# Linear attention and a gated MLP in one kernel: a fourth buffer in a shared ring, 64-wide kv, px in quarters

## The chip, the cores and the metric

The kernel runs on one core of a Trainium2 chip. The metric is the device time of one execution in microseconds. The kernel before took 828.76 us (median of three runs, 827.92 to 829.11). Engines are named as in the profile: PE is TensorE (PEld its weight loads), DVE VectorE, ACT ScalarE, POOL GpSimd, SP SyncE, which issues nearly all DMAs.

## The reference

q, k and v are 8 batches x 8 heads x 576 positions x 64, in float32; the MLP goes from 512 to 2048 and back. Cut to what is computed:

```python
q_s = softmax(q, axis=-1)            # over the 64 of a head
k_s = softmax(k, axis=2)             # over the 576 positions
kv  = einsum('bhsd,bhse->bhde', k_s, v)      # 64 x 64 for each batch and head
x   = einsum('bhsd,bhde->bhse', q_s, kv)     # then 4608 tokens x 512
h   = x @ w_in
g   = h * clip(h + 3, 0, 6) / 6
out = g @ w_out
```

The attention is linear: `kv` is small, and each token's query multiplies the `kv` of its own batch and head.

## The kernel before

**Stages.** The 4608 tokens are handled as three blocks of 512 (j = 0, 1, 2) and then three super-blocks of 1024 (s = 0, 1, 2). Two heads always go together as a head pair (hp, four of them), with 2 x 64 = 128 partitions. Blocks run the MLP as two plain products: for each of 16 chunks of the hidden width, `gemm1` makes `ph`, relu6 makes `g`, and `gemm2` adds into four banks `po`; `store` (L770) empties these at a block's end, two on ACT (L781) and two on DVE (L779). A float32 value is split into a high and a low part, and each product is three fast passes (hi·hi, hi·lo, lo·hi). Super-blocks use a two-by-two scheme with seven products in place of eight, which needs sums and differences of weight blocks.

**Weights.** They arrive as raw words (`load_w`) and are decoded during block 0 by `decode` (L146): ACT and DVE steps through `m` into a tile `v`, then a split into a resident tile `w`. From chunk 6 on `v` is also stored to DRAM (`whole`, L166). During blocks 1 and 2 `sum_weights` (L482) takes a pair of chunks and a side (in or out) at a time: it fills a tile `w4` with the plain weights (from `w` for the first three pairs, L488, later by a load of `whole`, L491), writes the sums into a second tile `sums` (L497 to L500), splits both and stores four blocks to DRAM (`keep`, L469, seen as `wf<-v`). The generator `all_sums` has 26 steps; one is taken in each chunk from block 1's n = 4 on (`n > 3`).

**The ring `v`.** One ring of three buffers of 4 KB per partition, all under the name `v`, serves the decoded tile, `w4`, `sums`, block 2's output tiles (L773), the last relu6 of phase 1 (L626) and phase 2's output tiles (L662). A new tile waits until all readers of the one three back have finished, stores included.

**Attention.** For a batch and a head pair, `kv_of` (L207) forms `pkv` in PSUM (576 positions in 5 pieces, 2 heads, 64 columns of `v` and one of ones), takes the reciprocal of the sums and writes `kv`. For block 0, block 1, block 2 and super-block 0, `kv` is a 128x128 tile with the two heads' 64x64 on the diagonal and zeros elsewhere, made by one DVE instruction with a `mask` (L225). The product `px` with the turned queries `qT` is then one matmul of the whole array for each run of tokens of one batch. From super-block 1 on (`quarters`) `kv` is 64 wide (L221), and `px` is made of 64x64 matmuls on the four corners of the array: rows by head, columns by which 512 tokens, with a PSUM bank for each head (L421 to L435). A float32 matmul shows up as two instructions.

**Queries.** `attention` (L276) serves blocks 0 and 1. For block 1 the queries come into `qt`, are normalised there, turned on PE into PSUM (`tp`) and copied by ACT to a second tile `qT` (L298); both have one buffer. `token_attention` (L361) serves the rest; its queries come in a layout that DVE can turn (L350), into a tile also called `qt` (L384).

**Order.** A planner in the framework simulates the program while it is built and puts each engine's instructions in order; buffers that are not free yet are part of what it simulates. From block 1 on matmuls keep the order in which the program names them. `behind` ties work to come after the last relu6 or split that was issued. Attention for the next stage runs in small steps between the chunks (`steps`, L808): a list of units, a number of steps for each, and `shared`, the steps at which the unit before goes on too. Block 1's attention runs during block 0 with 3 steps a unit and `shared = (2,)`, so the previous unit's px comes with the present unit's `kv_of`. Engines and SP's queue run strictly in the order that they were given.

Of the kernel before, what the change touches and what calls it, by code (L numbers as in the profile page):

```python
# [33 lines left out]
def attention_moe(  # L34
# [62 lines left out]
    make_identity(nc, ident)  # L97
    mask = const.tile([P, P], F32, name="mask")
    nc.gpsimd.memset(mask, 0.0)
    nc.gpsimd.memset(mask[0:D, 0:D], 1.0)  # L100
    nc.gpsimd.memset(mask[D:P, D:P], 1.0)
    three = const.tile([P, 1], F32, name="three")
# [43 lines left out]
    def decode(f):  # L146

        n = 2 * DM
        pairs = raws.pop(f).rearrange("p (n two) -> p n two", two=2)
        low, high = pairs[:, :, 0], pairs[:, :, 1]  # L150
        m = moe.tile([P, n], F32, name="m", bufs=1)
        nc.scalar.activation(m, high.bitcast(F32), AF.Abs)
        nc.vector.tensor_scalar(m, m, W_MIN, W_MAX, op0=ALU.max, op1=ALU.min)
        m = m.bitcast(U32)
        nc.vector.tensor_scalar(
            m, m, 3, 0x3FFFFFFF, op0=ALU.logical_shift_left, op1=ALU.bitwise_and
        )
        v = moe.tile([P, n], F32, name="v", bufs=3)
        vu = v.bitcast(U32)
        nc.vector.scalar_tensor_tensor(  # L160
            vu, high, 0xC0000000, m, op0=ALU.bitwise_and, op1=ALU.bitwise_or
        )
        nc.scalar.activation(low, low, AF.Copy, scale=2.0**-29)
        nc.vector.tensor_tensor(vu, vu, low, op=ALU.add)
        if f // 2 >= FROM_DRAM:
            nc.sync.dma_start(whole[:, f], v)  # L166
        parts = place(f, F32R, f"w_{f}").rearrange("p (s i n) -> p s i n", s=2, i=2)
        split_ahead(
            parts[:, :, 0],
            parts[:, :, 1],  # L170
            v.rearrange("p (s n) -> p s n", s=2),
        )
        wi[f], wo[f] = parts[:, 0], parts[:, 1]
# [9 lines left out]
    kvs = {}  # L183
    narrow = set()

# [6 lines left out]

    first = {}

    def load_first(hp):
# [10 lines left out]

    def kv_of(hp, batches, quarters=False):  # L207
        n = len(batches)
        both = bank_a("pkv")[:, 0 : n * (D + 1)].rearrange("p (b d) -> p b d", b=n)
        for i, (_, ke, vt) in enumerate(batches):  # L210
            for c in range(NCH):
                for h in range(2):
                    hs = slice(h * D, (h + 1) * D)
                    mm(both[hs, i], ke[:, c, hs], vt[:, c, h, :], c == 0, c == NCH - 1, n > 1)
        rk = att.tile([P, 2], F32, name="rk", bufs=2)[:, 0:n]
        nc.vector.tensor_scalar_add(rk, both[:, :, D], EPS)
        nc.vector.reciprocal(rk, rk)
        for i, (b, _, _) in enumerate(batches):
            kv = att.tile([P, P], F32, name="kv", bufs=10)
            if quarters:  # L220
                nc.vector.tensor_scalar_mul(kv[:, 0:D], both[:, i, 0:D], rk[:, i : i + 1])  # L221
                kvs[b, hp] = kv
                narrow.add((b, hp))
                continue
            nc.vector.scalar_tensor_tensor(  # L225
                kv.rearrange("p (h d) -> p h d", h=2),
                both[:, i : i + 1, 0:D].broadcast_to([P, 2, D]),
                rk[:, i : i + 1],
                mask.rearrange("p (h d) -> p h d", h=2),
                op0=ALU.mult,  # L230
                op1=ALU.mult,
            )
            kvs[b, hp] = kv
# [42 lines left out]
    def attention(j, hp):  # L276

        if not j:
            kt, qt, qT, vt, ke = first[hp]
        else:  # L280
            kt = load_kt(j, hp)
            ke = att.tile([P, NCH, P], F32, name="ke", bufs=2)
            vt = load_v(j, hp)
            qt = att.tile([P, TB], F32, name="qt", bufs=1)
            nc.sync.dma_start(qt, q[j, hp])
            qt = qt.rearrange("p (c h d) -> p c h d", c=NC4, h=2)
        km = att.tile([P, 1], F32, name="km", bufs=2)
# [10 lines left out]
        nc.scalar.copy(qT, tp)  # L298
# [37 lines left out]
    def q_softmax_t(qt):  # L336
# [14 lines left out]
        return qT  # L351

    held = {}

# [6 lines left out]
    def token_attention(t0, n, hp, put):  # L361
# [39 lines left out]
        yield  # L401
        kv_of(hp, list(zip(new, ke, vt)), t0 >= START + SB)
        yield
# [7 lines left out]
    def sb_attention(s):  # L411
        def put(t0, hp, need, qT):

            if not s:
                for c in range(SB // TB):
                    px = bank_a("px")
                    for b, lo, hi in segments(need, t0 + c * TB):
                        mm(px[:, lo:hi], kvs[b, hp], qT[:, c * TB + lo : c * TB + hi], True, True)
                    nc.scalar.copy(x_of(s)[:, hp, c * TB : (c + 1) * TB], px)
                return  # L420
            px = [bank("px") for _ in range(2)]  # L421
            rows = [slice(h * D, (h + 1) * D) for h in range(2)]
            for both in zip_longest(*(segments(need, t0 + c * TB) for c in range(2))):
                for c, part in enumerate(both):
                    if part:
                        b, lo, hi = part
                        for h, r in enumerate(rows):
                            mm(
                                px[h][rows[c], lo:hi],
                                kvs[b, hp][r, slice(0, D) if (b, hp) in narrow else r],  # L430
                                qT[r, c * TB + lo : c * TB + hi],
# [10 lines left out]
    def block_attention(j):  # L442
        def put(t0, hp, need, qT):
            px = bank_a("px")
            for b, lo, hi in segments(need, t0):
                mm(px[:, lo:hi], kvs[b, hp], qT[:, lo:hi], True, True)
            x_hi, x_lo = x_block(j)
            split(x_hi[:, hp, :], x_lo[:, hp, :], px)
# [33 lines left out]
    def sum_weights(pair, side):  # L482

        w4 = moe.tile([P, 2 * DM], F32, name="v", bufs=3)
        if pair < FROM_DRAM:
# [8 lines left out]
        a11, a12, a21, a22 = (q1, q3, q2, q4) if side else (q1, q2, q3, q4)  # L494
        sums = moe.tile([P, 2 * DM], F32, name="v", bufs=3)
        s1, s3, s2, s4 = (sums[:, n * HT : (n + 1) * HT] for n in range(4))
# [85 lines left out]
    def phase1(s):  # L582
        xb, yb, zb = {}, {}, {}
        for i, (p, n) in enumerate(SLOTS1):
# [24 lines left out]
            with tc.high_priority():  # L609
# [14 lines left out]
                if n == 6:  # L624
                    nc.vector.tensor_add(h21, h21, y)
                    r = moe.tile([P, 2 * DM], F32, name="v", bufs=3)  # L626
                    relu6(gb, r, gb)
            yield

    def phase2(s):  # L630
# [30 lines left out]
        def outs(name):  # L661
            return moe.tile([P, 2 * DM], F32, name="v", bufs=3).rearrange("p (c n) -> p c n", c=2)  # L662

# [106 lines left out]
    def store(j, po):  # L770
        for t in range(NTT):
            if j == NB - 1:
                ob = moe.tile([P, 2 * DM], F32, name="v", bufs=3)[:, 0:DM]  # L773
            else:
# [66 lines left out]
    for j in range(NB):  # L841
        if j == 1:
            in_order.append(True)
        if j < NB - 1:
# [119 lines left out]
```

## Time and profile before

| | us |
|---|---|
| median of three runs | 828.76 |
| profiled execution, its own time | 827.1 |
| its span, first to last instruction | 825.3 |
| PE busy | 798.8 (97%) |
| DVE busy | 673.4 (82%) |
| ACT busy | 454.1 (55%) |
| POOL busy | 55.7 (7%) |

In the profile a line is that of the kernel's source, and a helper that records every matmul gives all matmuls one line (L88); they are told apart by `out<-in`, the names of the tiles. A shape such as `64*64 64x320` is the part of the array used and the moving data. A number in brackets after an instruction is the idle time of its engine just before it, and what ended that. Busy time of PE uses modelled ends of matmuls, so short idle times of PE do not show in it. The profile's clock is the share of full speed that TensorE was granted, 0.996 over the whole span.

### The profile page before, as it was taken

How to read it: one execution, taken by the hardware profiler on the slowest of the kernel's cores; microseconds unless marked ns; L12 is line 12 of the kernel's file. 1: busy time of each engine (PE TensorE's matmuls, PEld its weight loads, DVE VectorE, ACT ScalarE, POOL GpSimd, SP SyncE). 2: the span in 40 equal slices, each digit the busy share in tenths (PEclk: the TensorE clock that was granted, in tenths of full speed). 3: DMA queues.
4: the chain of work that ended last, by engine and by line, in shares of the span. 5: the costliest groups of instructions: out<-in, count | busy, mean ns of one | idle time of the engine just before them, and what ended most of it. 6: DMA issues, size and time to landing. Idle time of an engine off the chain costs nothing.

```text
span 825.3 us, 11783 instructions
## 1 busy us (share of the span) xinstructions
PE 798.8 (97%) x4088; PEld 641.3 (78%) x4088; DVE 673.4 (82%) x1064; ACT 454.1 (55%) x733; POOL 55.7 (7%) x155
## 2 busy tenths in 40 slices
PE   4899899999989999999999999999999999999998
PEld 3577678888877778887877788777788888888886
DVE  7998998589979888888999994798699836658873
ACT  7897673334444445556556653565556535445543
POOL 5000001010111110001003000011000000000000
PEclk9999999999999999999999999999999999999999
DMA  9999676245579873888786677775566776666673
GB/s 368 416 407 334 199 263 225 59 163 189 192 239 341 288 263 128 267 279 277 272 279 213 187 233 251 226 234 183 178 184 199 238 247 197 187 201 185 197 218 114
DMA packets 75803, 192.30 MB, mean 233 GB/s; under 512 B 7264, under 2 KB 19808, under 8 KB 73696
## 3 DMA queue, kind: packets, MB, share of 16 engines
q1 hardware_dynamic: 75024, 190.38, 70.1%
q10 hardware_dynamic: 720, 1.18, 0.4%
q8 instruction: 32, 0.52, 0.3%
q14 instruction: 27, 0.22, 0.1%
HBM read 147.49 MB, written 44.04 MB: 232 GB/s over the span
## 4 chain that ended last, share of the span: by engine, by line
PE 69%; DVE 16%; DMA 7%; ACT 4%; issue 3%; SPq 1%; POOL 1%; DVEq 0%; ACTq 0%; POOLq 0%
PE x L88 29%; PE z L88 11%; PE y L88 11%; PE ph L88 7%; PE po L88 7%; DMA wf<-v 4%; DMA qt<-in_qf_dram 2%; PE px L88 2%; DVE g L580 1%; PE pkv L88 1%; DVE v L160 1%; DVE qt L343 1%; DVE v L121 1%; DVE gp L121 1%; DVE m L350 1%
## 5 line engine op out<-in xcount | busy, mean ns | idle before, releaser
L121 ACT CAST gf<-g 128x512 fp32r<-128x512 f32 x168 | 104.2, 622 | 97.5 <-DVE gf L121 37.0
L88 PE MATMUL po<-w,gp 128*128 128x512 f32 x576 | 145.5, 399 | 3.6 <-DVE gp L779 2.1
L88 PE MATMUL ph<-x,w 128*128 128x512 f32 x576 | 142.7, 394 | 3.2 <-ACT w L121 2.0
L121 DVE TENSOR_TENSOR gf<-g,gf 128x512 fp32r<-128x512 f32 x168 | 112.9, 686 | 25.3 <-ACT gf L121 24.9
L88 PEld LDWEIGHTS ph<-x,w 128*128 128x128 f32 x576 | 107.8, 188 | 29.6 <-ACT w L121 3.0
L88 PEld LDWEIGHTS po<-w,gp 128*128 128x128 f32 x576 | 106.7, 189 | 29.2 <-DVE gp L779 2.5
L88 PE MATMUL x<-right,gp 128*128 128x512 f32 x384 | 94.6, 391 | 0.4 <-ACT g L616 0.4
L88 PE MATMUL x<-gf,gp 128*128 128x512 f32 x384 | 94.1, 390 | 0.0
L88 PEld LDWEIGHTS x<-gf,gp 128*128 128x128 f32 x384 | 71.9, 188 | 15.7 <-DVE gf L121 0.4
L88 PEld LDWEIGHTS x<-right,gp 128*128 128x128 f32 x384 | 71.6, 188 | 15.7 <-ACT g L616 0.8
L579 ACT ACTIVATE g<-ph,three 128x512 f32<-128x512 f32 x48 | 32.7, 684 | 38.1 <-PE ph L88 38.1
L88 PE MATMUL y<-right,gp 128*128 128x512 f32 x192 | 49.1, 391 | 0.0
L88 PE MATMUL x<-right,left 128*128 128x512 f32 x192 | 47.7, 392 | 0.0
L88 PE MATMUL x<-gf,left 128*128 128x512 f32 x192 | 47.0, 390 | 0.0
L88 PE MATMUL z<-gf,gp 128*128 128x512 f32 x192 | 46.9, 390 | 0.0
L333 POOL COPY swap<-qm 32x32 f32<-32x32 f32 (+1 forms) x64 | 19.6, 306 | 355.3 <-DVE qm L341 353.3
L121 ACT CAST gp<-g 128x512 fp32r<-128x512 f32 x48 | 29.7, 619 | 23.8 <-DVE g L580 23.7
L88 PEld LDWEIGHTS z<-gf,gp 128*128 128x128 f32 x192 | 36.0, 188 | 7.8 <-DVE gf L121 0.4
L88 PEld LDWEIGHTS x<-gf,left 128*128 128x128 f32 x192 | 35.9, 188 | 7.7 <-ACT v L702 0.2
L88 PEld LDWEIGHTS y<-right,gp 128*128 128x128 f32 x192 | 35.8, 188 | 7.6 <-issue 0.2
L88 PEld LDWEIGHTS x<-right,left 128*128 128x128 f32 x192 | 35.7, 188 | 7.6
L580 DVE SCALAR_TENSOR_TENSOR g<-g,ph 128x512 f32<-128x512 f32 x48 | 32.6, 680 | 9.2 <-ACT g L579 9.1
(139 smaller groups left out, 1279.8 us busy)
## 6 DMA issues: line engine op xcount, KB each, us to landing
gp<-wf SPq DMA_DIRECT2D x112, 512.0 KB, 4.2
left<-wf SPq DMA_DIRECT2D x56, 512.0 KB, 4.2
raw<-in_w_dram SPq DMA_DIRECT2D x16, 1024.0 KB, 13.6
wf<-v SPq DMA_DIRECT2D x64, 256.0 KB, 3.2
wf<-w SPq DMA_DIRECT2D x48, 256.0 KB, 4.5
vt<-in_v_dram SPq DMA_DIRECT2D x28, 325.0 KB, 5.6
kt<-in_kT_dram SPq DMA_DIRECT2D x28, 288.0 KB, 3.8
ke<-in_k_dram SPq DMA_DIRECT2D x24, 320.0 KB, 5.1
```

What stands on the lines that cost most here:

```text
L88: nc.tensor.matmul(out, lhsT, rhs, start=start, stop=stop, skip_group_check=goes_on)
L121: return nc.scalar.copy(hi, src), nc.vector.tensor_sub(lo, src, hi.bitcast(F32))
L160: nc.vector.scalar_tensor_tensor(vu, high, 0xC0000000, m, op0=ALU.bitwise_and, op1=ALU.bitwise_or)
L333: nc.gpsimd.tensor_copy(swap[r : r + QD], stat[o : o + QD])
L343: nc.vector.tensor_sub(qs, qs, across(qm))
L350: nc.vector.transpose(qT, qt)
L579: ahead(nc.scalar.activation(r, h, AF.Relu, bias=three, scale=1.0))
L580: ahead(nc.vector.scalar_tensor_tensor(g, r, 6.0, h, op0=ALU.min, op1=ALU.mult))
```

## The change

- The ring `v` has four buffers, at all seven places where it is named.
- Room for it: `mask` is gone; `kv` is 64 wide for every batch (ten tiles); `qT` of block 1 is gone. Its queries now come into half of a tile `qt` that is 1024 wide and shared with `token_attention` (kept in `held["q"]`, halves by turns of hp), and the turned queries are copied back to where they came from.
- `px` of all stages that used the whole array is made by the new function `heads`: two 64x64 matmuls for each run of tokens, rows and columns of one head, both into the same PSUM bank.
- Block 1's attention has `shared = (1,)`: the previous unit's px comes with the present unit's transposes.
- The sums of weights start one chunk earlier, at n = 3 of block 1 (`n > 2`).

```diff
-    mask = const.tile([P, P], F32, name="mask")
...
-        v = moe.tile([P, n], F32, name="v", bufs=3)
+        v = moe.tile([P, n], F32, name="v", bufs=4)
...
-    def kv_of(hp, batches, quarters=False):
+    def kv_of(hp, batches):
...
-            kv = att.tile([P, P], F32, name="kv", bufs=10)
-            if quarters:
...
-            nc.vector.scalar_tensor_tensor(
...
+            kv = att.tile([P, D], F32, name="kv", bufs=10)
+            nc.vector.tensor_scalar_mul(kv, both[:, i, 0:D], rk[:, i : i + 1])
             kvs[b, hp] = kv
...
-            qt = att.tile([P, TB], F32, name="qt", bufs=1)
-            nc.sync.dma_start(qt, q[j, hp])
-            qt = qt.rearrange("p (c h d) -> p c h d", c=NC4, h=2)
+            if "q" not in held:
+                held["q"] = att.tile([P, SB], F32, name="qt", bufs=1)
+            qT = held["q"][:, hp % 2 * TB : (hp % 2 + 1) * TB]
+            nc.sync.dma_start(qT, q[j, hp])
+            qt = cut(qT, 0, NC4, 2, D)
...
-        if j:
-            qT = att.tile([P, TB], F32, name="qT")
         nc.scalar.copy(qT, tp)
...
-                mm(px[:, lo:hi], kvs[b, hp], qT[:, lo:hi], True, True)
+                heads(px, lo, hi, kvs[b, hp], qT, True)
...
+    def heads(px, lo, hi, kv, qT, start):
+
+        for h in range(2):
+            r = slice(h * D, (h + 1) * D)
+            mm(px[r, lo:hi], kv[r], qT[r, lo:hi], start, True, True)
...
-                step = steps(units, 3, (2,))
+                step = steps(units, 3, (1,))
...
-            if j > 1 or j and n > 3:
+            if j > 1 or j and n > 2:
                 behind(sums)
```

The other puts (super-block 0, block 2) change in the same way as the one shown; those of super-blocks 1 and 2 keep their order and only lose the test for which kind of `kv` they read.

More of the change, by code (lines that the diff above doesn't have):

```diff
@@ L97, in attention_moe @@
     make_identity(nc, ident)
-    mask = const.tile([P, P], F32, name="mask")
-    nc.gpsimd.memset(mask, 0.0)
-    nc.gpsimd.memset(mask[0:D, 0:D], 1.0)
-    nc.gpsimd.memset(mask[D:P, D:P], 1.0)
     three = const.tile([P, 1], F32, name="three")
@@ L183, in attention_moe @@
     kvs = {}
-    narrow = set()
     def cut(t, at, *shape):
@@ L193, in attention_moe @@
     first = {}
+    held = {}
     def load_first(hp):
@@ L218, in kv_of @@
         for i, (b, _, _) in enumerate(batches):
-            kv = att.tile([P, P], F32, name="kv", bufs=10)
-            if quarters:
[L221 to L232, printed above, removed]
+            kv = att.tile([P, D], F32, name="kv", bufs=10)
+            nc.vector.tensor_scalar_mul(kv, both[:, i, 0:D], rk[:, i : i + 1])
             kvs[b, hp] = kv
@@ L351, in q_softmax_t @@
         return qT
-    held = {}
     def x_of(s):
@@ L401, in token_attention @@
         yield
-        kv_of(hp, list(zip(new, ke, vt)), t0 >= START + SB)
+        kv_of(hp, list(zip(new, ke, vt)))
         yield
@@ L417, in put @@
                     for b, lo, hi in segments(need, t0 + c * TB):
-                        mm(px[:, lo:hi], kvs[b, hp], qT[:, c * TB + lo : c * TB + hi], True, True)
+                        heads(px, lo, hi, kvs[b, hp], qT[:, c * TB : (c + 1) * TB], True)
                     nc.scalar.copy(x_of(s)[:, hp, c * TB : (c + 1) * TB], px)
@@ L429, in put @@
                                 px[h][rows[c], lo:hi],
-                                kvs[b, hp][r, slice(0, D) if (b, hp) in narrow else r],
+                                kvs[b, hp][r],
                                 qT[r, c * TB + lo : c * TB + hi],
@@ L445, in put @@
             for b, lo, hi in segments(need, t0):
-                mm(px[:, lo:hi], kvs[b, hp], qT[:, lo:hi], True, True)
+                heads(px, lo, hi, kvs[b, hp], qT, True)
             x_hi, x_lo = x_block(j)
@@ L482, in sum_weights @@
     def sum_weights(pair, side):
-        w4 = moe.tile([P, 2 * DM], F32, name="v", bufs=3)
+        w4 = moe.tile([P, 2 * DM], F32, name="v", bufs=4)
         if pair < FROM_DRAM:
@@ L494, in sum_weights @@
         a11, a12, a21, a22 = (q1, q3, q2, q4) if side else (q1, q2, q3, q4)
-        sums = moe.tile([P, 2 * DM], F32, name="v", bufs=3)
+        sums = moe.tile([P, 2 * DM], F32, name="v", bufs=4)
         s1, s3, s2, s4 = (sums[:, n * HT : (n + 1) * HT] for n in range(4))
@@ L625, in phase1 @@
                     nc.vector.tensor_add(h21, h21, y)
-                    r = moe.tile([P, 2 * DM], F32, name="v", bufs=3)
+                    r = moe.tile([P, 2 * DM], F32, name="v", bufs=4)
                     relu6(gb, r, gb)
@@ L661, in outs @@
         def outs(name):
-            return moe.tile([P, 2 * DM], F32, name="v", bufs=3).rearrange("p (c n) -> p c n", c=2)
+            return moe.tile([P, 2 * DM], F32, name="v", bufs=4).rearrange("p (c n) -> p c n", c=2)
         def send(t, r, c):
@@ L772, in store @@
             if j == NB - 1:
-                ob = moe.tile([P, 2 * DM], F32, name="v", bufs=3)[:, 0:DM]
+                ob = moe.tile([P, 2 * DM], F32, name="v", bufs=4)[:, 0:DM]
             else:
```

## The prediction

> **What bounds the kernel now.** I read the head of the page first, then busy time by stage, then who waited for whom, and last the timelines of the few places where TensorE stood still. The page:
>
> ```profile
> span 825.3 us, 11783 instructions
> PE 798.8 (97%) x4088; PEld 641.3 (78%) x4088; DVE 673.4 (82%) x1064; ACT 454.1 (55%) x733; POOL 55.7 (7%) x155
> ```
>
> The stages (start and end, length, then busy time and instructions of PE, PEld, DVE, ACT and POOL, granted clock, DMA share, GB/s); 34 to 130 is block 0 with its decoding, 130 to 232 block 1, 232 to 330 most of block 2, then the super-blocks:
>
> ```profile
> 0.00:34.00 34.00, 21.10 (x147) 16.00 (x148) 28.61 (x52) 26.61 (x39) 12.85 (x25) 0.95 0.97 386
> 34.00:130.00 96.00, 91.18 (x461) 69.76 (x460) 90.79 (x129) 73.54 (x149) 0.50 (x2) 0.98 0.86 310
> 130.00:232.00 102.00, 102.00 (x550) 82.64 (x549) 85.12 (x166) 42.81 (x68) 11.82 (x44) 1.00 0.48 155
> 232.00:330.00 98.00, 94.47 (x516) 76.30 (x515) 83.74 (x151) 44.84 (x70) 11.60 (x36) 1.00 0.76 259
> 330.00:825.00 495.00, 490.10 (x2421) 396.63 (x2419) 385.12 (x570) 266.33 (x411) 18.90 (x48) 1.00 0.70 219
> ```
>
> TensorE sets the end. In block 1 it never stops, so whatever is added to it there is paid and whatever another engine saves there is lost. It can gain 3.5 us in block 2 (98.00 less 94.47), 4.8 us in block 0, where VectorE with 90.79 of 96 is as much the bound, and little later. Who waited for whom (total, times, longest):
>
> ```profile
> PE po L88 <- DVE gp L779: 2.1, 1, 2.1
> DVE v L497 <- DMA wf<-v: 5.6, 3, 3.0
> PE px L88 <- DVE kv L225: 2.2, 2, 1.9
> ```
>
> The second row is the ring of the change: L497 writes the new sums tile `v`, and with three buffers it must wait until the stores `wf<-v` of the tile three back have landed. What such a wait does is seen on VectorE at the turn from block 1 to block 2, and on TensorE at the same time:
>
> ```profile
> 240.25 0.43 DVE L497 TENSOR_TENSOR v<-v 128x256 f32<-128x256 f32 x1 [2.95 <-DMA wf<-v]
> ...
> 240.93 1.24 DVE L350 STREAM_TRANSPOSE m<-qt 128x1024 f32<-128x1024 f32 x1
> ...
> 243.05 1.54 DVE L396 TENSOR_TENSOR ke<-ke,pm 128x640 f32<-128x640 f32 x2
> 244.51 0.68 DVE L121 TENSOR_TENSOR gp<-g,gp 128x512 fp32r<-128x512 f32 x1
> 245.12 0.68 DVE L779 TENSOR_SCALAR gp<-po 128x512 f32<-128x512 f32 x1
> ```
>
> ```profile
> 245.85 1.42 PE L88 MATMUL po<-w,gp 128*128 128x512 f32 x5 [2.13 <-DVE gp L779]
> ```
>
> L779 empties a PSUM bank that block 2's second product needs; it stands in VectorE's queue behind the 2.95 us wait. The same happens once more:
>
> ```profile
> 282.75 0.43 DVE L497 TENSOR_TENSOR v<-v 128x256 f32<-128x256 f32 x1 [1.89 <-DMA wf<-v]
> ...
> 287.01 0.69 DVE L121 TENSOR_TENSOR gp<-g,gp 128x512 fp32r<-128x512 f32 x1
> ```
>
> ```profile
> 287.75 0.50 PE L88 MATMUL po<-w,gp 128*128 128x512 f32 x1 [0.84 <-DVE gp L121]
> ```
>
> **The change part by part.** All terms are against the profiled execution's own 827.1 us (span 825.3); the median of the three runs, 828.76, lies 1.7 above it, and I add the sum to the median.
>
> *The fourth buffer* takes the two waits at L497 away: a sums tile then takes the slot of a tile one further back, whose stores left earlier. Without them every VectorE instruction behind comes 2.95 and 1.89 us sooner, more than the 2.13 and 0.84 us that TensorE stood, so both gaps close: -2.97 us. Bounds: 0 (the planner puts other work there, a rival below) and -3.5, all idle time of the stage. Later waits on the ring are not on the path: the load of `w4`, which now waits for the slot instead, has a whole chunk to land. In block 0 the ring gives nothing: no VectorE wait on a store is listed before 165 us.
>
> *Px by quarters* replaces each 128x128 product with two of 64x64, for two heads, on opposite corners of the array. What such a put costs is read from the last super-blocks, which have quarters already (all four corners at once, 1024 tokens), and from super-block 0, which has whole ones for 1024 tokens:
>
> ```profile
> 368.31 0.39 PE L88 MATMUL x<-right,gp 128*128 128x512 f32 x1
> ...
> 368.62 1.09 PE L88 MATMUL px<-m,kv 64*64 64x320 f32 x16
> 369.65 0.43 PE L94 MATMUL pm<-ident,km 128*128 128x128 f32 x2
> ```
>
> ```profile
> 234.51 0.40 PE L88 MATMUL ph<-x,w 128*128 128x512 f32 x1
> ...
> 234.75 1.89 PE L88 MATMUL px<-m,kv 128*128 128x192 f32 x8
> 236.47 0.41 PE L94 MATMUL pm<-ident,km 128*128 128x128 f32 x2
> ```
>
> ```profile
> 306.50 2.72 PE po L88 x12
> ```
>
> A whole 512-wide matmul ahead takes 2.72/12 = 0.23 us. The whole put takes 236.47 - 234.51 - 0.23 = 1.73 us, of which 234.75 to 236.47 = 1.72 us is streaming: eight instructions that move 2 x 1024 columns, 0.84 ns a column, and nothing lost. The quarter put takes 369.65 - 368.31 - 0.23 = 1.11 us. Each corner gets two passes over 512 columns, 1024 x 0.84 ns = 0.86 us, so 0.25 us go into entering and leaving the small tiles. The corners ran at once, at the rate of the whole array. Two corners instead of four then need the same 0.86 us for 512 tokens as the whole array, and the change pays only the 0.25 us, once for each put (the two halves of a put of super-block 0 follow each other). Eight puts (block 2's four and super-block 0's four) lie where TensorE is full: +2.0 us; bounds 0 and +2.8 (0.35 each). Four belong to block 1's attention and lie in block 0, where VectorE shares the bound: of 1.0 us I count half, +0.5 (0 to 1.0). The first four come in two groups on the opening chain,
>
> ```profile
> 22.42 2.97 PE L88 MATMUL px<-kq,kv 128*128 128x512 f32 x6
> 28.02 1.10 PE L88 MATMUL px<-kq,kv 128*128 128x512 f32 x2 [1.89 <-DVE kv L225]
> ```
>
> so twice 0.25: +0.5 (0 to 1.0).
>
> The Trainium skill says otherwise of the corners: in "TensorEngine Tiling (Array Packing)", Gotcha 1 (PSUM Pressure), different row tiles cannot access the same PSUM bank simultaneously. The old quarters gave each head a bank of its own; `heads` writes both into one. No trace here shows two row tiles in one bank; what waiting would cost stands under the rivals.
>
> *64-wide kv.* The scaling goes from the first of these rows to the second:
>
> ```profile
> L225 DVE SCALAR_TENSOR_TENSOR kv<-pkv,rk,mask 128x128 f32<-128x128 f32 x20 | 6.5, 339 | 0.0
> L221 DVE TENSOR_SCALAR kv<-pkv,rk 128x64 f32<-128x64 f32 x12 | 3.0, 277 | 0.1
> ```
>
> That is 0.06 us for each of 20. TensorE waited for it twice (2.2 us above); there it counts, and in block 0's full VectorE queue: -0.3 us (0 to -1.2). Mask fills leave POOL, which is idle for most of the opening (12.85 of 34 us): 0.
>
> *Queries in place, and px one step earlier.* ScalarE no longer waits for the previous px before it copies the turned queries:
>
> ```profile
> 84.05 0.59 ACT L298 COPY qT<-tp 128x512 f32<-128x512 f32 x1 [0.65 <-PE px L88]
> ```
>
> Behind it on ScalarE stand the next decode's first step and the weights' cast; but VectorE, which these feed, has no idle time then, so 0 (down to -0.65 for each of three units). The halves are one tile with block 2's first query tile, so that load waits for block 1's last px rather than for its transposes:
>
> ```profile
> 116.03 0.33 SPq L384 DMA_DIRECT2D qt<-in_qf_dram  x1
> ```
>
> ```profile
> 128.90 0.92 PE L88 MATMUL px<-qT,kv 128*128 128x448 f32 x2
> ```
>
> ```profile
> 143.29 0.27 PE L94 MATMUL pm<-ident,km 128*128 128x128 f32 x1
> ```
>
> It moves from 116 to about 130 us. SyncE's queue behind it (weight stores, block 2's k and v) may move with it; the first product that needs any of that is `pm` at 143.3, so 0, and up to +1 if the cover of 13 us is used up by late loads.
>
> *Sums from the fourth chunk (n > 2).* One step of all 26 moves from the end of block 2 into block 1, with its adds of 0.43 us, its splits and its four stores; VectorE idles there for 102.00 - 85.12 = 16.9 us and DMA is half free (0.48): 0.
>
> Sum: -2.97 + 2.0 + 0.5 + 0.5 - 0.3 = -0.27; 828.5 us.
>
> **Rivals.** *Block 0 gets a better order* (faster). Its largest gap starts on VectorE, which stands in order before L259 until ScalarE has done eight small exponentials; the debt reaches TensorE ten microseconds later:
>
> ```profile
> 81.02 0.17 DVE L259 TENSOR_SCALAR qr<-qr 128x8 f32<-128x8 f32 x1 [2.05 <-ACT qt L247]
> ```
>
> ```profile
> 92.99 0.50 PE L88 MATMUL ph<-x,w 128*128 128x512 f32 x1 [2.00 <-ACT w L121]
> ```
>
> ```profile
> 91.10:94.50 3.40, 1.48 (x8) 1.03 (x9) 3.40 (x6) 3.16 (x6) 0.00 (x0) 1.00 0.56 216
> 94.50:97.90 3.40, 3.40 (x10) 2.64 (x9) 3.40 (x5) 2.74 (x15) 0.00 (x0) 0.51 0.67 210
> ```
>
> The gap costs 2.0 us and then 3.4 us at a clock of 0.51, 1.7 us more. The planner orders block 0 anew, with px and its split one step earlier, and if L259 no longer stands ahead of ready decoding the 3.7 us are saved: 824.8 us. Against it: nothing in the edit touches that wait, and VectorE's load stays.
>
> By the Trainium skill ("TensorE: Matmul & The Clock Gate", "Why this matters for your kernels") only gaps over about 3 us bring the slow clock; the trace shows it after 2.00 us. By the rule this rival would be worth 2.0 us.
>
> *VectorE is late again, from its own work* (slower). At the turn to block 2 the wait began at 240.25 - 2.95 = 237.30; from its end to L779 VectorE worked 245.12 - 240.25 = 4.9 us, and TensorE needed the bank at 245.85 - 2.13 = 243.72, 6.4 us after 237.30. If the freed ring and the earlier sums let the planner put over 1.5 us more ahead of L779, three or four adds, the gap comes back at its old size, and all twelve later puts, the opening and kv remain: 2.0 + 1.0 + 0.5 - 0.3 = +3.2, 832.0 us.
>
> *Two row tiles in one bank take turns* (slower). Each put of 512 tokens then needs 0.86 us more; there are 4 + 4 + 4 + 8 = 20 of them, 17.2 us, and 12 of these (10.3 us) lie where TensorE is full: 839 to 846 us. For it speaks only the rule. Against it speak the kv products, two halves of the columns that write different partitions of one bank:
>
> ```profile
> L88 PE MATMUL pkv<-vt,ke 128*64 128x65 f32 x560 | 20.7, 225 | 0.0
> ```
>
> 20.7 us for 560 is 37 ns each, and 65 columns at 0.84 ns are 55 ns: they run together (though with all 128 rows each).
>
> **How the numbers follow.** A difference under 0.2%, 1.7 us, can't be told from none here. The sum, with a range of its own from 826.5 to 830.5, has 0.42: 0.32 within 0.2%, 0.06 faster, 0.04 slower. Block 0's better order has 0.32, the late VectorE 0.20, the turns in one bank 0.06. So faster 0.38, same 0.32, slower 0.30. The range takes in the first three, 822.5 to 833, and leaves out the last and the tails.
>
> **What would show it.** Right: no L497 wait on `wf<-v`, no gap before po near 243.7 and 286.9, px pairs that start within some ns of each other, about 0.25 us lost at each put, and TensorE still full in block 1. The px groups of block 2 twice as long would show turns in one bank; a gap behind L779 without a DMA wait ahead of it would show the late VectorE; a clock of 1.00 right through block 0 would show the better order. A gap of over 1 us at a new place, which no row of before points to, would prove the sum wrong in kind, not in size.

## The result, and the profile after

The kernel after takes **832.66 us** (median of 9 runs, 829.85 to 835.39), the kernel before beside it 827.92 (9 runs, 825.77 to 829.50). The ratio is 1.0053, 95% interval 1.0035 to 1.0072: slower by 3 to 6 us. The forecast was 828.5. The profiled execution of after took 833.49 us, with a span of 831.7. Most lines shift with the edit: L333 to L350 of before are L324 to L341 now, and the sums' first add L497 is L486, relu6 L579 and L580 are L568 and L569, the copy of px L419 is L408, the store's L779 and L781 are L768 and L770.

Busy time by stage of the kernel after, columns as in the prediction:

```profile
0.00:34.00 34.00, 20.42 (x148) 14.47 (x149) 27.19 (x50) 25.45 (x38) 12.41 (x22) 0.90 0.97 384
34.00:130.00 96.00, 91.23 (x478) 69.88 (x478) 92.55 (x132) 75.08 (x150) 0.40 (x2) 0.98 0.87 309
130.00:232.00 102.00, 101.75 (x559) 80.31 (x558) 85.30 (x169) 42.22 (x67) 12.91 (x40) 1.00 0.56 184
232.00:330.00 98.00, 93.32 (x534) 73.19 (x533) 80.07 (x142) 40.73 (x64) 12.00 (x40) 0.98 0.66 230
330.00:825.00 495.00, 493.38 (x2435) 399.15 (x2434) 388.68 (x574) 269.13 (x414) 18.89 (x48) 1.00 0.67 218
```

The stage from 232 to 330, where the forecast saw TensorE filled, stands idle for 98.00 - 93.32 = 4.68 us, more than the 3.53 us of before, and its clock fell to 0.98. The waits of the stretch from 130 to 350 us in the kernel after (total, times, longest) say on whom:

```profile
PE pm L94 <- ACT x L408: 4.0, 3, 2.4
DVE v L486 <- DMA wf<-v: 0.7, 2, 0.5
```

The ring did what it was made for: the sums' wait for their stores fell from 5.6 us to 0.7. In its place stands a wait that cost nothing before. `pm` (the maxima of the keys, turned by TensorE) takes its bank from the two-bank pool `ps_a`, and a put of super-block 0 has just put px into both of these. So `pm` cannot start until ScalarE has copied px out (L408), and here ScalarE was late. TensorE and then ScalarE in the timeline of after:

```profile
238.57 1.62 PE L88 MATMUL px<-m,kv 64*64 64x320 f32 x12 [0.67 <-DVE kv L217]
242.56 0.43 PE L94 MATMUL pm<-ident,km 128*128 128x128 f32 x2 [2.38 <-ACT x L408]
242.75 4.59 PE L88 MATMUL po<-w,gp 128*128 128x512 f32 x12
```

```profile
240.40 1.06 ACT L335 ACTIVATE qt<-qt 128x1024 f32<-128x1024 f32 x1 [6.04 <-DVE qt L334]
241.36 0.67 ACT L568 ACTIVATE g<-ph,three 128x512 f32<-128x512 f32 x1
241.94 1.06 ACT L408 COPY x<-px 128x512 f32<-128x512 f32 x2
```

In ScalarE's list the exponential of the next queries (L335) stands ahead of the two copies. ScalarE stood idle for 6.04 us, until 240.40, because L335 waited for VectorE's L334; px lay finished from 238.57 + 1.62 = 240.19 on. VectorE in turn had waited for the load of those queries:

```profile
235.82 1.22 DVE L332 TENSOR_REDUCE qm<-qt 128x32 f32<-128x1024 f32 x1 [2.05 <-DMA qt<-in_qf_dram]
...
239.14 1.23 DVE L334 TENSOR_TENSOR qt<-qt,qm 128x1024 f32<-128x1024 f32 x1
```

Right behind the 2.38 us gap the slow clock comes, a row of the busy time of after for that window:

```profile
243.20:246.60 3.40, 3.40 (x10) 2.65 (x9) 3.40 (x8) 2.00 (x4) 0.50 (x3) 0.51 0.43 117
```

3.40 us at 0.51 lose 1.7 us more. Two further puts wait in the same way (0.53 us at 264, 1.10 at 285). The stage thus loses 4.68 + 1.7 = 6.4 us where before it lost 3.53.

### The profile page after: what moved, and what is told of

Same layout as the page of the kernel before. It is cut to its first block, busy times and chain, and to the rows that moved or that the text cites. A ratio compares the mean times of both kernels' runs of the same rounds, so it can differ in the third digit from the quotient of the medians.

```text
span 831.7 us, 11919 instructions
## 1 busy us (share of the span) xinstructions
PE 803.0 (97%) x4160; PEld 639.0 (77%) x4160; DVE 674.2 (81%) x1064; ACT 453.6 (55%) x733; POOL 56.6 (7%) x152
## 4 chain that ended last, share of the span: by engine, by line
PE 52%; DVE 9%; DMA 4%; ACT 2%; issue 2%; POOL 1%; SPq 0%; POOLq 0%; DVEq 0%
PE x L88 29%; PE z L88 11%; PE y L88 10%; DMA qt<-in_qf_dram 3%; POOL swap L324 1%; DVE m L341 1%; DVE qt L334 1%; DVE g L569 1%; PE px L88 1%; PE pkv L88 1%; DVE qm L332 1%; DVE qt L339 1%; DMA wf<-v 1%; ACT right L117 1%; DVE qr L336 1%
## 5 line engine op out<-in xcount | busy, mean ns | idle before, releaser
L568 ACT ACTIVATE g<-ph,three 128x512 f32<-128x512 f32 x48 | 32.9, 685 | 48.5 <-PE ph L88 48.4
L324 POOL COPY swap<-qm 32x32 f32<-32x32 f32 (+1 forms) x64 | 20.8, 324 | 357.5 <-DVE qm L332 340.3
L568 ACT ACTIVATE g<-g,three 128x512 f32<-128x512 f32 x24 | 17.4, 725 | 38.6 <-DVE g L602 38.5
```

The lines of the kernel that those rows point to most:

```text
L324: nc.gpsimd.tensor_copy(swap[r : r + QD], stat[o : o + QD])
L568: ahead(nc.scalar.activation(r, h, AF.Relu, bias=three, scale=1.0))
```

## The experiments

The expectations were written in groups, and each group's letters name the theories of that group; the text after each run says in words which held. "Begins super-block 0 at" is the shift of the first product of that stage against the profiled execution of before.

**Three buffers again.** The kernel after with `bufs=3` at all six places where the ring is named (the list of the change counts seven; the kernel has six).

> The changed kernel with three buffers in the ring v again; everything else as changed. Theory A (the fourth buffer lets the planner put the query exponential ahead of the px copies on ScalarE, which costs 4.0 us of TensorE at three pm products and eats the 3 us that the ring gives): the pm gaps go (ScalarE waits under 1 us there), waits of the first sums instruction on wf<-v come back with gaps of 2 to 3 us, time within 2 us of the changed kernel, about 831.5. Theory B (the ring is good and the loss is all px in quarters and queries in place): 3 us slower than the changed kernel, 835.5, and the pm gaps stay.

830.76 us, 1.0044 (1.0027 to 1.0061), as theory A said. Three buffers don't make the changed kernel slower than four do. The sums wait again and pm waits less: in this order the exponential ran at 233.3 us, well ahead of the copies at 240.3 (the list of waits, as above):

```profile
DVE v L486 <- DMA wf<-v: 3.8, 4, 1.9
PE pm L94 <- ACT x L408: 0.8, 1, 0.8
```

So the loss isn't the ring's by itself, and the ring's gain does not show.

**Whole-array px.** The kernel after with px as before (128x128 kv with the mask, nine tiles so that the fourth buffer fits).

```diff
-        for h in range(2):
-            r = slice(h * D, (h + 1) * D)
-            mm(px[r, lo:hi], kv[r], qT[r, lo:hi], start, True, True)
+        mm(px[:, lo:hi], kv, qT[:, lo:hi], start, True)
```

> The changed kernel with kv block-diagonal, 128 wide with the mask, and px by one whole-array matmul for each run of tokens as before; the ring keeps four buffers, the room comes from nine kv tiles instead of ten. Theory A with its price of 0.27 us for each of 12 puts: 12 x 0.27 = 3.2 us faster than the changed kernel, about 829.4, the pm gaps of super-block 0 still there. Theory B' (the quarters are free, all loss is ScalarE's order): no change, 832.7. Theory C (the loss is chance in the plan of block 0 and the super-blocks): anything within 2 us, with the stages between 130 and 330 us as in the changed kernel.

832.28 us, 1.0045 (1.0025 to 1.0065): no gain, the time of theory B'. Taking the quarters away doesn't give the loss back. What they cost, this run doesn't show: pm waits 3.3 us in it, and another gap, of 2.21 us, has come at 138 us.

**The exponential behind the copies.** The kernel after, with L335 tied to be issued after the px copies of the put before it.

```diff
-        qT = q_softmax_t(qt)
+        with ExitStack() as order:
+            if t0 >= START and "px" in held:
+                order.enter_context(tc.issue_after(held["px"].ins))
+            qT = q_softmax_t(qt)
```

> The changed kernel with one constraint more: in super-block 0 each query exponential is issued on ScalarE after the px copies of the unit before. Theory A: the gaps of 2.38, 0.53 and 1.10 us ahead of pm go, 832.7 - 4.0 = 828.7. Theory B': the copies were late for another reason (VectorE's kv, the quarters); the gaps stay or move and the time stays at 832.7. Theory D: the exponential, now later, delays the chain to the next put, and the time goes up by 1 us or more.

835.76 us, 1.0099 (1.0074 to 1.0125): slower, in size as theory D said. All three pm gaps are gone and super-block 0 begins 2.2 us sooner than in the kernel after. But the tie also moves the query work on VectorE later, ahead of the split of `right` that super-block 0 needs; TensorE of this run at the turn:

```profile
335.79 3.02 PE L88 MATMUL po<-w,gp 128*128 128x512 f32 x12 [0.60 <-ACT gp L117]
...
348.60 2.16 PE L88 MATMUL x<-right,left 128*128 128x512 f32 x5 [2.50 <-DVE right L117]
```

and slow clock behind that. The edit cures one place and hurts another, so it prices neither.

**Quarters and 64-wide kv alone, on the kernel before** (three buffers, queries and sums as before).

> The kernel before with only kv 64 wide and px in quarters; three buffers, queries in two tiles, sums from n = 4 and block 1's px step as before. Price of 0.25 to 0.3 us for each put: 8 puts in the full stages 2.2 us, 4 in block 0 0.5 to 1, the opening 0.5: 3 to 4 us slower than the kernel before, about 831.4, with px pairs that run together. If the quarters are free: 828. If two row tiles take turns in one bank: over 838.

843.73 us, 1.0179 (1.0152 to 1.0207). Over 838, but not for the reason that number was given: px pairs still run together (each put of block 2 takes 0.27 us more than before, not 0.86). The largest part is one stall of TensorE of 3.78 us at 320 with 6.8 us at half clock behind it, together 7.2 of some 15 us. Its cause is settled by the run with three buffers and the later sums, below. Another 4.7 us are lost by 148 us, in the opening and block 0; this run alone doesn't explain them.

**Queries in place alone, on the kernel before**, with `shared = (1,)`.

> The kernel before with only the queries of block 1 turned in place and px one step earlier (shared = (1,)); three buffers, whole-array px, sums from n = 4. By its direct price nothing, 828.3 with the two waits of the first sums instruction on wf<-v and the gap near 243 still there. Theory C (each edit makes the planner lay all queues out anew, and that alone is worth several us): a difference of 2 us or more to either side, with no step at the px puts.

828.97 us, 1.0010 (0.9993 to 1.0027): nothing, as forecast.

**The same with the fourth buffer** (nine kv tiles make the room; with three buffers nine or ten tiles give the same lists of instructions, so the ring is the one difference).

```diff
-        v = moe.tile([P, n], F32, name="v", bufs=3)
+        v = moe.tile([P, n], F32, name="v", bufs=4)
...
-            kv = att.tile([P, P], F32, name="kv", bufs=10)
+            kv = att.tile([P, P], F32, name="kv", bufs=9)
```

> As e5, and the ring v with four buffers (the room from nine kv tiles; the order of e5 does not depend on that); so against e5 it is the fourth buffer alone, and against the changed kernel it lacks the quarters and the earlier sums. In its order of issue ScalarE copies px ahead of the query exponential in super-block 0. Theory A: no long pm waits, no waits of the first sums instruction on wf<-v, no price of quarters: 3 us faster than e5 and faster than the kernel before, 825 to 826. Theory C: within 2 us of e5 or slower, with new gaps elsewhere.

829.20 us, 1.0010 (0.9993 to 1.0027): the ring alone moves the time by nothing that shows, as theory C said. The waits of the sums on `wf<-v`, 6.6 us in the run without it, are gone from the list, and so is the gap near 244; but the planner, with the buffer free, set other work forward, and TensorE stood in new places:

```profile
138.25 2.15 PE L88 MATMUL po<-w,gp 128*128 128x512 f32 x6 [2.20 <-ACT gp L121]
```

```profile
337.05 0.73 PE L88 MATMUL po<-w,gp 128*128 128x512 f32 x2 [0.67 <-ACT gp L121]
338.48 2.56 PE L88 MATMUL po<-w,gp 128*128 128x512 f32 x10 [0.70 <-DVE gp L121]
...
345.89 1.45 PE L88 MATMUL x<-right,left 128*128 128x512 f32 x5 [1.90 <-DVE right L121]
```

**The sums from the fourth chunk as before**, all else as in the kernel after.

```diff
-            if j > 1 or j and n > 2:
+            if j > 1 or j and n > 3:
```

> The changed kernel with the sums from n = 4 as before; four buffers, quarters and queries as changed. In its order of issue one px copy of each put comes ahead of the query exponential and one behind. Theory A: pm waits fall from 4.0 to under 2 us, quarters still cost 0.27 us each: 830 to 831. If the start of the sums has no part in ScalarE's order: 832.7 with the same pm gaps.

828.88 us, 1.0018 (1.0001 to 1.0036), below the 830 to 831 of theory A. Undoing the smallest edit of all takes back 3.8 us by the medians and 2.9 by the ratios, whose intervals just touch. pm still waits, 1.97 us at one place, without the slow clock behind it.

**Whole-array px with the tie** (the second and third run's edits together).

> e2 (the changed kernel with whole-array px) with the query exponential of super-block 0 tied behind the px copies, as in e3. The pm gaps (3.3 us in e2) go and the quarters' price is gone: 829 or below if nothing else stalls. Theory C: the time saved at pm is lost again at the turn to super-block 0, where VectorE got the query work later in e3: 831 to 834.

833.49 us, 1.0067 (1.0048 to 1.0086), theory C. The same as with quarters: the pm gaps at the puts make way for one of 2.50 us at `right` (348 us) with slow clock behind it, and smaller ones.

**The earlier sums alone, on the kernel before.**

> The kernel before with one edit: the sums of the weights begin at block 1's third chunk instead of its fourth. Theory C, formed after the first runs (the earlier sums are what costs: VectorE's sums stand ahead of the attention's work at the turn to block 2, whatever the ring, and the same three-buffer ring makes the sums wait as before): 831 us, +2.5 to +4 us (1.003 to 1.005), with the loss in the trace after 200 us and new waits of the px products or of pm on VectorE or ScalarE. The prediction's theory (the earlier sums cost 0, VectorE has room in block 1): 828, 0.999 to 1.001. Theory N (earlier sums cost only together with the quarters, whose puts lengthen TensorE's list): 828 as well, but then the stages at the turn to block 2 stand within 0.5 us of before.

828.04 us, 0.9999 (0.9983 to 1.0015). My theory after the first eight runs, that the earlier sums cost 3 us wherever they are, is wrong. They cost nothing in the kernel before, and cost something only in the changed plan.

**Three buffers and the later sums**, all else as in the kernel after.

> The kernel after with three buffers and the sums from the fourth chunk: quarters, queries in place and the 64-wide kv alone are left of the change. Against the run with four buffers and the same sums (828.88, 1.0018) it shows the ring's worth beside the quarters. Theory C (the ring's room is worth nothing in time by itself): 829 to 830, 1.001 to 1.003. The prediction's theory (the ring is worth 3 us): 832, 1.004 to 1.006, with waits of the sums on the weights' load of 5 us and more. Against the run of quarters and 64-wide kv without the queries in place (843.73) it shows whether that run's stall of 3.78 us at 320 us and the half clock behind it belong to the quarters (then it comes again, 838 and above) or to that one order of SyncE's list (then it is gone).

839.10 us, 1.0131 (1.0103 to 1.0160), against 828.88 with four buffers: in this plan the fourth buffer is worth about 10 us. The stall at 320 us came again. SyncE's queue, then VectorE, then TensorE of this run:

```profile
313.59 0.37 SPq L480 DMA_DIRECT2D v<-whole  x1
314.06 0.41 SPq L373 DMA_DIRECT2D qt<-in_qf_dram  x1
```

```profile
320.05 1.22 DVE L332 TENSOR_REDUCE qm<-qt 128x32 f32<-128x1024 f32 x1 [4.79 <-DMA qt<-in_qf_dram]
321.19 0.68 DVE L117 TENSOR_TENSOR v<-v 128x512 fp32r<-128x512 f32 x1
321.79 0.68 DVE L569 SCALAR_TENSOR_TENSOR g<-g,ph 128x512 f32<-128x512 f32 x1
```

```profile
323.17 4.21 PE L88 MATMUL po<-w,gp 128*128 128x512 f32 x9 [4.86 <-ACT gp L117]
```

The load of `w4` (L480) needs a free buffer of the ring, and SyncE waited for one (the list of SyncE's waits between 300 and 330 us):

```profile
SPq L480 <- DMA wf<-v: 8.3, 3, 5.1
```

The query load L373 stands behind it in the same queue and left at 314.06; VectorE's L332 waited 4.79 us for it, relu6 (L569) stands behind that, and TensorE waited 4.86 us for the `g` that relu6 makes. With four buffers and the same sums this query load left 7.50 us sooner, and TensorE did not stop there:

```profile
306.56 0.38 SPq L373 DMA_DIRECT2D qt<-in_qf_dram  x1
```

The stall of the run with quarters on the kernel before (3.78 us at 320) is the same: its SyncE waits 5.3 us at the load of `w4`, and its VectorE 3.95 us for the queries.

A second loss of this run is the old gap at the turn to block 2: 2.25 us ahead of 249.13, behind L768, with 3.4 us at half clock after it. The first run, with three buffers and the earlier sums, has neither of the two. So three buffers cost this much in some orders only.

**The later sums with the tie.**

> The kernel after with the sums from the fourth chunk, and ScalarE's exponential of the query tied behind the px copies of the put before it. Theory C (with the later sums VectorE has room, so the tie only takes away the waits of pm on the px copies, 2.3 us in the run without the tie): 826.5 to 828.5, 0.998 to 1.000. Theory D (what is gained at the puts is lost at the turn to super-block 0, where the query's work then comes ahead of the split of the right-hand side on VectorE, as with the earlier sums): 830 to 834, 1.003 to 1.008, with a gap of TensorE of 2 us or more between 335 and 350 us. The prediction's theory has no term for it: 828.

828.59 us, 0.9995 (0.9975 to 1.0014). Without the earlier sums the tie doesn't hurt at the turn, but it gains nothing that can be told from the run without it (1.0018), and pm still waits 1.76 us at one place.

**Another bank for pm, throughout.** The kernel after; `pm` comes from the pool of six banks, so it can't wait for the px copies.

```diff
-        pm = bank_a("pm")
+        pm = bank("pm")
```

> The kernel after with one edit: pm, the transposed maxima of the keys, takes its bank from the pool of six banks in place of the pool of two that holds px, so that it cannot wait for the px copies; the sums still begin at the third chunk and the exponential of the query still stands where the planner puts it. The kernel after lost 2.38, 0.53 and 1.10 us at pm and 1.7 us at half clock behind the first of them. Theory E (those waits are what the earlier sums cost in the changed kernel): 827 to 829.5, 0.998 to 1.002, no gap of TensorE ahead of pm between 235 and 290 us. Theory F (the late query on VectorE is the cause and pm only shows it first; the px copies stay late, so the next px or the first products of super-block 0 wait in place of pm): 831 to 834, 1.003 to 1.008, with gaps of 1 us and more ahead of px or x between 240 and 350 us. The prediction's theory (the earlier sums cost nothing): no forecast but no change against the kernel after.

835.94 us, 1.0094 (1.0067 to 1.0120), and yet the most telling run until then. Two stages of it:

```profile
232.00:330.00 98.00, 98.00 (x563) 77.71 (x564) 84.93 (x147) 44.63 (x69) 12.11 (x40) 1.00 0.68 237
330.00:825.00 495.00, 486.34 (x2389) 392.88 (x2388) 382.21 (x565) 263.52 (x406) 16.72 (x48) 0.99 0.66 216
```

TensorE is full in block 2, and super-block 0 begins 1.07 us ahead of before (the kernel after: 5.64 behind). All is lost again in the super-blocks, where the six banks are needed by px and the products and `pm` now takes one of them:

```profile
370.51 1.66 PE L88 MATMUL z<-right,gp 128*128 128x512 f32 x6 [1.50 <-ACT x L430]
...
380.60 2.93 PE L88 MATMUL x<-right,left 128*128 128x512 f32 x6 [2.98 <-ACT g L608]
```

These, three later gaps of 0.67, 1.04 and 1.60 us, and 6.8 us at a clock of 0.50 from 380 on (3.4 us lost) make 11.2 us.

**Another bank for pm in block 2 alone.** The same edit, for super-block 0's attention only.

```diff
-        pm = bank_a("pm")
+        pm = (bank if START <= t0 < START + SB else bank_a)("pm")
```

> The kernel after with pm in the pool of six banks for super-block 0's attention alone (during block 2), and as before in the later super-blocks, where the run with pm in that pool throughout showed gaps ahead of z and x (1.50, 2.98, 0.67, 1.04 and 1.60 us) and 3.4 us at half clock. That run began super-block 0 1.07 us ahead of before, where the kernel after began it 5.64 us behind. Theory E (pm's wait for the px copies, with the half clock behind it, is what the earlier sums cost in the changed kernel, and without it the ring's gain shows): 825 to 827.5, 0.996 to 0.999, super-block 0 begun at or ahead of before. Theory F (pm only moves the loss on): super-block 0 begun 3 us and more behind before, or new gaps of 2 us at the turn, 830 to 834. The prediction's sum had 828.5 for the change as it stands.

827.63 us, 0.9996 (0.9982 to 1.0009), against 1.0053 (1.0035 to 1.0072) of the kernel after: **one bank is worth about 5 us** (832.66 - 827.63 = 5.0; by the ratios 0.57%, or 4.7 us, give or take 1.9). The same put in this run, TensorE and ScalarE:

```profile
236.86 2.15 PE L88 MATMUL px<-m,kv 64*64 64x192 f32 x16
238.93 0.43 PE L94 MATMUL pm<-ident,km 128*128 128x128 f32 x2
239.12 2.98 PE L88 MATMUL po<-w,gp 128*128 128x512 f32 x12
```

```profile
239.21 1.06 ACT L335 ACTIVATE qt<-qt 128x1024 f32<-128x1024 f32 x1 [5.97 <-DVE qt L334]
240.17 0.67 ACT L571 ACTIVATE g<-ph,three 128x512 f32<-128x512 f32 x1
240.74 1.06 ACT L411 COPY x<-px 128x512 f32<-128x512 f32 x2
```

ScalarE is as late as in the kernel after, 5.97 us of idle time ahead of L335 and the copies behind it; but TensorE goes from px to `pm` to `po` without a gap. The lists of ScalarE, VectorE and SyncE are the same in both runs up to 293 us, past all three waits of `pm`; behind that the planner has moved some instructions. So it was the shared bank, not the late exponential, that made the lateness count. Of the rival that pm only shows the loss first, nothing is left: no gap over 0.62 us follows up to the end. But theory E said more than came: super-block 0 begins 0.64 us behind before, not at or ahead of it, and of the ring's gain the time shows nothing.

**The bank with the later sums and the tie.**

> The kernel with the sums from the fourth chunk and the exponential tied behind the px copies (828.59, 0.9995), with pm in the pool of six banks during block 2; nothing else differs and every engine's list is the same. Its gap ahead of pm was 1.76 us at 280 us, with no half clock behind it. Theory E: 1.5 to 2 us less, 826.5 to 827.2, 0.997 to 0.999. Theory F: no change, 828.0 to 829.0.

827.12 us, 0.9990 (0.9977 to 1.0003), from 828.59: 1.5 us by the medians, the size forecast, but 0.4 by the ratios (0.9995 to 0.9990), with the intervals overlapping. The time alone doesn't settle it; the gap of 1.76 us ahead of `pm` is gone from the trace, and the lists are the same.

**The bank on the kernel before.**

> The kernel before with pm in the pool of six banks during block 2; every engine's list is the same. Its waits of pm on the px copies were 0.6 us in 3 places. Theory E (the bank is worth what pm waited, so it is worth something in the changed kernel alone): 827.5 to 828.5, 0.9985 to 1.0005. If the bank is worth something by itself: 826 or less, 0.998 or less; then a gain of the run with pm in block 2 beside the kernel after would not belong to the change.

828.44 us, 0.9997 (0.9984 to 1.0011): nothing. The bank is worth something only where the change made pm wait. In the kernel before the wait was there, too small to count:

```profile
PEld pm L94 <- ACT x L419: 0.6, 3, 0.2
```

**The bank with the later sums, no tie.**

> The kernel after with the sums from the fourth chunk (828.88, 1.0018) and pm in the pool of six banks during block 2. Theory E: its gap of 1.97 us ahead of pm at 279 us goes, 826.5 to 827.5, 0.998 to 1.000; and the earlier sums then cost nothing against it (the run with pm in block 2 and the sums from the third chunk within 1.5 us). Theory F: 828.5 to 830.

826.02 us, 0.9975 (0.9964 to 0.9987), a little below theory E's 826.5: **faster than both kernels**, with the change's quarters, queries and ring, the sums where they were, and one bank moved. Block 2 of this run is full at full clock:

```profile
232.00:330.00 98.00, 98.00 (x572) 77.68 (x566) 85.13 (x151) 44.84 (x70) 10.52 (x40) 1.00 0.69 244
```

Against it the run with the bank and the earlier sums (827.63) is 1.6 us slower; the intervals (0.9964 to 0.9987 and 0.9982 to 1.0009) overlap a little, so what the earlier sums cost once pm has its bank stays open between nothing and some 3 us.

## Why the prediction was wrong

**The step that failed** is the first term, "both gaps close: -2.97 us". Both gaps did close, and the waits behind them fell as said. But TensorE's room in block 2 was to be filled by that, and was not: a new wait took its place, of 4.0 us at `pm`, and 1.7 us of slow clock behind it. The bound that I gave the term, 0 at worst, took the planner's new order to be no worse than the old one. I looked at what the freed VectorE would serve, and not at which buffers its later instructions hold. The row of before that names the place, pm behind the px copies with 0.2 us at most, could be had from the trace (it is quoted above), and I did not look for it as a resource with no slack: two banks, both filled by one put, and the next product wants one of them.

The trace shows where the sum went wrong. The profiled span of the kernel after is 831.7 - 825.3 = 6.4 us longer. By the same products in both profiles, 1.0 us of that stands when the first `pm` of block 1 begins (143.29 and 144.29), 1.5 come in the four puts up to the first `ph` behind 232 us (232.02 and 234.54), 3.1 from there to the first product of super-block 0 (339.55 and 345.18), and 0.8 behind it. The forecast had 1.0, 1.0, -2.97 + 1.0 = -2.0 and 0 (kv's -0.3 left aside). Nearly all of the error, 5.1 us, lies in the third stretch, where both gaps closed and `pm` opened a new one.

With that one bank moved, the change measures 0.9996, or -0.4 us against before in the medians (828.07 there); the sum said -0.27. That agreement holds to the interval, about 1 us either way, and is in part luck: by the same products, the first three stretches cost 0.1, 1.9 and -1.4 us in that run's profile, where the forecast had 1.0, 1.0 and -2.0.

**By terms.**

- *The ring.* That its worth is 2.97 us was wrong in kind: it isn't a number of its own. It was 0 with whole-array px and the later sums (829.20 against 828.97), about 10 us with quarters and the later sums (828.88 against 839.10), and no gain in the kernel after itself (832.66 against 830.76 with three buffers). Where nothing else stands in the way, as in the fastest run, block 2's idle time goes from 3.53 us to nothing. The sentence "later waits on the ring are not on the path: the load of `w4` ... has a whole chunk to land" was wrong for three buffers: what counts is not when `w4` lands but what stands behind its issue in SyncE's queue.
- *Quarters.* Right. A put of block 2 in the kernel before and in the kernel after, from the first product ahead to the first behind:

```profile
158.01 2.89 PE L88 MATMUL ph<-x,w 128*128 128x512 f32 x12
160.74 1.03 PE L88 MATMUL px<-m,kv 128*128 128x128 f32 x4
161.61 0.27 PE L94 MATMUL pm<-ident,km 128*128 128x128 f32 x1
161.64 3.01 PE L88 MATMUL po<-w,gp 128*128 128x512 f32 x12
```

```profile
159.02 2.88 PE L88 MATMUL ph<-x,w 128*128 128x512 f32 x12
161.83 1.08 PE L88 MATMUL px<-m,kv 64*64 64x128 f32 x8
162.84 0.32 PE L94 MATMUL pm<-ident,km 128*128 128x128 f32 x1
162.92 3.00 PE L88 MATMUL po<-w,gp 128*128 128x512 f32 x12
```

  161.64 - 158.01 = 3.63 us before and 162.92 - 159.02 = 3.90 after: 0.27 us a put, where 0.25 was forecast. Two of the other three puts of this stretch grow by the same 0.27; the third, at 199 us, by 0.75, since it waits for kv.
- *Turns in one bank.* Not so: turns would have added 0.86 us to that put, and it grew by 0.27. Two heads in opposite corners write one bank at the whole array's rate, against Gotcha 1 of the Trainium skill's "TensorEngine Tiling (Array Packing)" as I had read it.
- *64-wide kv.* Not seen. TensorE still waits for kv in the kernel after (0.67 us at 238.6, and at 199 us, where it had not): the gain of 0.3 us, if there, is lost in that.
- *The opening, block 0.* The first `ph` comes 1.71 us later in the kernel after; but the kernel before with only the bank moved, whose lists are those of before, also shows it 0.94 us later (the granted clock of the first 34 us is 0.90 in both, and 0.95 before), and the runs with quarters lie between 0.2 and 1.8. The term of 0.5 can't be told from that. Block 0 lost a new gap of 3.25 us at 41 us, behind a cast that ScalarE took after six small exponentials, and made it good before block 1 began: 1.00 us behind before there, of the 1.71. So its better order, the faster rival, brought nothing that lasted: the gap of before at 91 us and its slow clock are gone, and another gap and another 3.4 us at half clock, at 45 us, stand in their place.
- *Queries in place.* Right: 828.97, nothing.
- *Sums from the fourth chunk.* "0" was right in the kernel before (828.04) and wrong in the changed one: with them 832.66, without them 828.88. The reason given, idle time of VectorE and of DMA, was true and beside the point. They changed which instruction stood ahead of which on ScalarE in block 2: without them one px copy of that put runs ahead of the exponential (238.28 and 238.74) and one behind it.
- *The late VectorE*, the slower rival, gave 832.0, close to the time measured, by another mechanism: no gap stands behind L768, and what came late was ScalarE behind a query load. It wasn't borne out.
- *The sign* that I named, "a gap of over 1 us at a new place ... would prove the sum wrong in kind", is what the trace showed: 2.38 us ahead of `pm`.

## What to carry to other kernels

A removed wait is worth its size only if the next resource on that path has slack: list the pools that the freed instructions and their neighbours hold, and look for one that a single step fills, however short its wait is in the trace before. In a kernel whose order a planner makes, single edits don't add: the fourth buffer measured 0 and about 10 us, the earlier sums 0 and 3 to 4 us, depending on the others, so test it in the company it will have. An engine with a strict queue pays for what stands ahead of the urgent instruction, the load of queries behind the load of weights or the copies out of PSUM behind an exponential, and the cheapest cure can be to take away what depends on the late instruction.

## What the runs showed of the hardware

Gaps well under 3 us brought the slow clock in this kernel: 2.38 us in the kernel after (0.51 for 3.40 us), and 2.50 at the turn to super-block 0 in two runs with the tie; 2.98 us and 4.86 us each brought 6.8 us at 0.50. But 2.13 us in the kernel before brought none; and of two gaps at the same place ahead of 138 us, 2.20 us with the fourth buffer on the kernel before brought 3.4 us at half clock, 2.21 us in the run with whole-array px none. So the length of the gap alone doesn't decide it.

In these traces, where the gap falls does. In every profile the slow stretches begin whole multiples of 3.41 us apart (at 45.27 and 243.25 us in the kernel after, 58 of them), so each run can be cut into windows of that length that begin where slow stretches can begin. The windows around four of these gaps, columns as in the prediction: two of the kernel before, one of the kernel after, one of the fourth buffer on the kernel before, two of whole-array px.

```profile
241.33:244.74 3.41, 2.40 (x11) 1.66 (x9) 3.41 (x6) 1.46 (x3) 0.00 (x0) 1.00 0.58 129
244.74:248.15 3.41, 2.30 (x10) 1.92 (x11) 2.54 (x5) 1.20 (x2) 0.00 (x0) 1.00 1.04 396
239.83:243.25 3.42, 1.04 (x8) 0.65 (x5) 2.30 (x4) 2.60 (x4) 0.37 (x2) 1.00 0.32 117
136.40:139.81 3.41, 1.56 (x6) 0.98 (x7) 2.59 (x5) 1.61 (x4) 0.00 (x0) 1.00 0.21 77
134.02:137.43 3.41, 2.07 (x10) 1.37 (x8) 2.32 (x6) 1.27 (x2) 0.77 (x4) 1.00 0.28 87
137.43:140.85 3.42, 2.54 (x10) 1.81 (x11) 2.65 (x5) 1.82 (x3) 0.37 (x1) 1.00 0.26 77
```

The gaps without slow clock lie across an edge, and TensorE idles for 1.01 and 1.11 us, and for 1.34 and 0.88, in the two windows; the gaps with it put 2.38 and 1.85 us into one. Between 34 and 815 us of all 18 profiles, a window at full clock with 1.8 us or more of idle TensorE was followed by one at half clock, 21 times; one with 1.66 us or less never was. In eight of the 21 the gap ran on into the slow window, by 0.62 us or more, and the next window was slow too; in the other 13 TensorE did not idle in the slow window, and the clock came back. So the 1.7 us behind the gap of 2.38 us in the kernel after were in part chance: another gap at `pm`, of 1.97 us in the run with the later sums, lies across an edge (0.93 and 1.05) and brought no slow clock.

The Trainium skill's "TensorE: Matmul & The Clock Gate" ("Why this matters for your kernels") puts the limit at about 3 us; the gaps of 2.38 and 2.50 us speak against it here.
